# Exchanged weight groups as one transfer each, and a new pair in the shared slot

## The chip, the cores and the metric

The kernel runs on one core of a Trainium2 chip. The metric is the device time of one execution in microseconds (us). For the kernel before it is the median of three timed runs; the rows of the profile come from one further execution.

## The reference, cut to what matters

Two independent attention layers are computed and laid side by side in the output. Part A is a dilated sliding-window attention over 2048 positions. Part B, which the change touches, is a recurrent one: 2048 positions in 64 segments of 32, each with 8 memory rows in front that the segment before has made.

```python
for s in range(n_seg):                       # 64 segments
    h = concatenate([mem, xs])               # 8 memory rows + 32 rows, 640 wide
    q, k, v = h @ Wq, h @ Wk, h @ Wv         # 32 heads of 192
    p = softmax(mask(q @ k.T * scale))
    o = (p @ v) @ Wo                         # back to 640
    mem, out = o[:8], o[8:]                  # the next segment needs mem
```

Each of the four weights of part B has 640 x 6144 numbers in bf16, 7.9 MB; the four together do not fit in SBUF.

## The kernel before, in words

Part A comes first, and the weights of part B are loaded and copied while it runs. Then `segment(s)` (line 714) is called 64 times, and `project_late` (line 827) projects what was kept of the last rows.

**Groups and units.** The heads stand in four groups, 0 to 3. A group of Wq, Wk or Wv is five units `(m, g, dc)`, one for each fifth of the 640 input rows: a tile of 128 partitions x 1536 bf16, 3072 bytes in each partition, 384 KB in all. A group of Wo is six units `("o", i, 0)` of 128 x 1280, 320 KB each. Line 327 (`pieces`) lists the units of a group.

**Residents and exchanges.** Nearly all units stay in SBUF. For k, v and o, groups 0 and 3 (`SHARED`, line 305) share slots. Even segments take the groups in the order 0, 1, 2, 3 and odd ones 3, 2, 1, 0 (`TURN`, line 304). So the shared group that a segment uses first is used up early, its slots are overwritten with the other shared group, which the segment uses last and the next one first. `change` (line 376) does this with one `replace` (line 370) for each unit: the slot gets the new unit's name, and SyncE (the queue SP in the profile) issues a DMA from a copy in DRAM (`wcopy_...`, made by `copy_shared`, line 350). A DMA on SP waits until TensorE has read the old unit for the last time, and everything behind it on SP waits too.

**The pair.** `PAIR` (line 306) names two more units that share one slot: `("k", 1, 4)` and `("o", 17, 0)`, the latter belonging to group 2 of Wo. Each segment overwrites k's with o's after k of group 1 has been projected, and back after the output projection of group 2. That makes 5 + 5 + 6 + 2 = 18 weight loads in a segment.

**The order of a segment.** `ORDER` (line 294) is written out by hand and fixes the order on TensorE, VectorE, ScalarE and SP. A token is a step and the place in the turn: `k.0` projects k for the first group of the turn. Cut to the steps that the prediction uses:

```text
q.0 k.0 k.1 q.1 S.0 v.0 q.2 S.1 k.2 tp.0 v.1 q.3 mix.0 tp.1 S.2 k.3
out.0.0 v.2 out.0.1 mix.1 S.3 tp.2 v.3 mix.2 out.1.0 out.1.1 tp.3 out.2.0 out.2.1 mix.3 last ql
```

A projection (line 517, in `project32`) walks through the five units `dc`, with 4 matmuls for a unit, or 8 in the groups that a segment renews (it then projects later rows ahead). `out.0.0` multiplies the first four units of Wo of the first group (line 669), `out.0.1` the last two; `last` does all six of the last group (line 696). The first projection of the next segment, `q.0`, is preceded by `ql`.

**What SP issues in a segment, in order:** the four stores of the segment before (line 733, at `q.0`); five units of k after `k.0`; one unit of the pair after the k of group 1; the next input rows (`XS`, line 490) ahead of `v.0`; five units of v after `v.0`; six units of o after `out.0.1`; the other unit of the pair after the output of group 2. GpSimd issues the stores of `late_o` (line 654) on a queue of its own. The last segment also loads fifteen tiles of `late_o` (line 820) at `q.0`, `q.1` and `q.2`, and six units of Wo at `v.1` (line 822).

Of the kernel before, what the change touches and what calls it, by code (L numbers as in the profile page):

```python
# [8 lines left out]
BF16 = mybir.dt.bfloat16  # L9
# [293 lines left out]
SPREAD = "SSVV"  # L303
TURN = (0, 1, 2, 3), (3, 2, 1, 0)
SHARED = (0, 3)
PAIR = ("k", 1, 4), ("o", 17, 0)
LEAD_IN = 114


# [7 lines left out]
def part_b(ctx, tc, B_x, B_mem0, B_Wq, B_Wk, B_Wv, B_Wo, out, ident, n_seg, pre, mid):  # L317
    nc = tc.nc
# [8 lines left out]
    def pieces(m, g):  # L327
        if m == "o":
            return [("o", i, 0) for i in range(6 * g, 6 * g + 6)]
        return [(m, g, dc) for dc in range(5)]  # L330

    def unit_src(u):
        m, c, dc = u
        return wo_v[:, c] if m == "o" else w_in[m][:, dc, 1536 * c:1536 * c + 1536]

    def unit_cols(u):
        return 1280 if u[0] == "o" else 1536

    def two_rows(v, u):
        return v.rearrange("p (k d) -> p k d", k=2) if u[0] == "o" else v  # L340
# [7 lines left out]
    copied = {}  # L348

    def copy_shared():  # L350

        for u in [u for g in SHARED[::-1] for m in "kvo" for u in pieces(m, g)] + list(PAIR):
            copied[u] = dpool.tile([128, unit_cols(u)], BF16, name="wcopy_%s%d_%d" % u)[:]
            nc.sync.dma_start(two_rows(copied[u], u), unit_src(u))

    need = [(m, g) for m, g in (("q", 0), ("k", 0), ("q", 1), ("k", 1), ("q", 2), ("k", 2), ("v", 0), ("v", 1), ("o", 0),
                                ("q", 3), ("v", 2), ("o", 1), ("o", 2))]
    resident = [u for m, g in need for u in pieces(m, g) if u != PAIR[1]]
    res, slots, wait = {}, {}, set()

    def place_resident(pool, units):
        for u in units:
            slots[u] = pool.tile([128, unit_cols(u)], BF16, name="wres_%s%d_%d" % u)[:]
            res[u] = slots[u]

    def load_resident(units):
        for u in units:
# [2 lines left out]
    def replace(old, new):  # L370
        slots[new] = slots.pop(old)
        del res[old]
        res[new] = slots[new][:, 0:unit_cols(new)]
        nc.sync.dma_start(res[new], copied[new])

    def change(m, g):
        for old, new in zip(pieces(m, g), pieces(m, SHARED[0] + SHARED[1] - g)):
            replace(old, new)

    n_pre, used = 0, 0  # L380
    while n_pre < len(resident) and used < pre:
# [4 lines left out]
    dpool = ctx.enter_context(tc.tile_pool(name="b_copy", bufs=1, space=bass.MemoryType.DRAM))  # L386
# [4 lines left out]
    def window_rows(j):  # L391
        xj = x2[:, 160 * j:160 * j + 160].rearrange("(s n) d -> s n d", n=SEG)
        last = n_seg - 3
        return [(XW[0, j, 0:M], mem2[:, 160 * j:160 * j + 160]),
                (XA[j].rearrange("(t n) d -> t n d", n=M), xj[0:4, SEG - M:SEG]),
                (XW[1:last, j, 0:M], xj[4:n_seg, SEG - M:SEG]),
                (XW[last:n_seg, j, 0:M], xj[last:n_seg, SEG - M:SEG]),
                (XW[:, j, M:SEG], xj[:, 0:SEG - M])]

    rows = [window_rows(j) for j in range(4)]  # L400
# [87 lines left out]
    def load_x(s):  # L488
        if s < n_seg:
            nc.sync.dma_start(XS[:], XW[s].rearrange("j n c -> (j n) c"))  # L490
# [60 lines left out]
    def project_qk(s, m, g):  # L551
        return project32([ahead, main] if renewed(s, m, g) else [main], m, g)
# [13 lines left out]
    def values(s, g):  # L566
        return project32([ahead, main] if renewed(s, "v", g) else [main], "v", g)
# [146 lines left out]
    def segment(s):  # L714
        last = s + 1 == n_seg
        engine = {"S": S_, "V": V_}
        got = {}

        def project(m, g):
            if m == "v":  # L720
                got["v", g] = values(s, g)
            else:
                got[m, g] = project_qk(s, m, g)

        turn = TURN[s % 2]

        def step(name, *at):
            n = int(at[0][-1]) if at else None
            g = turn[n] if at else None
            if name in "qkv":  # L730
                if name == "q" and n == 0:
                    while stores:
                        nc.sync.dma_start(*stores.pop(0))
                if name == "v" and n == 0:
                    load_x(s + 1)
                project(name, g)
                if name != "q" and n == 0:
                    change(name, g)
                if (name, g) == PAIR[0][0:2]:
                    replace(*PAIR)  # L740
                if s == 0 and n == 0 and name != "q":
                    load_all("o", 1 if name == "k" else 2)
                if last and name == "q" and n < 3:
                    load_late(range(5 * n, 5 * n + 5))
                if last and name == "v" and n == 1:
                    load_outputs()
            elif name == "e":
                m = at[0][0]
                got["sb", m, g] = evacuate(m, got.pop((m, g)), [engine[c] for c in EVACUATE[at[0]]])
            elif name == "T":  # L750
                m = at[0][0]
                keep = fill_late(s, m, g, got.pop(("sb", m, g)))
                turn_in_place(columns_of(m, 0, 32))
                if at[0] == "k0" and s and keep:
                    got["keep"] = keep
                elif keep:
                    keep()
                if at[0] == "k1" and "keep" in got:
                    got.pop("keep")()
            elif name == "S":  # L760
                got["S", g] = scores(g)
            elif name == "sb":
                got["t", g] = soft_begin(got.pop(("S", g)))
            elif name == "mx":
                got["mx", g] = soft_max(got["t", g])
            elif name == "sub":
                soft_exp(got["t", g], got.pop(("mx", g)))
            elif name == "send":
                soft_end(s, g, got.pop(("t", g)))
            elif name == "tp":  # L770
                got["p", g] = turn_p(g)
            elif name == "PT":
                got["PT", g] = spread_p(got.pop(("p", g)), SPREAD[n])
            elif name == "ve":
                keep_values(g, got.pop(("v", g)))
            elif name == "mix":
                got["mix", g] = mix(g, got.pop(("PT", g)))
            elif name == "ot":
                keep_mix(s, g, got.pop(("mix", g)), [engine[c] for c in HEADS[n]])
            elif name == "out":  # L780
                half = int(at[1])
                if "Y" not in got:
                    got["Y"] = ps_y.tile([128, 320], FP32, tag="y", name="Y")
                n = int(at[0])
                g = turn[n]
                project_out(got["Y"], g, range(4 * half, 4 + 2 * half), n == 0, n == 2)
                if half and n == 0 and not last:
                    change("o", g)
                if half and g == PAIR[1][1] // 6 and not last:
                    replace(*PAIR[::-1])  # L790
            elif name == "part":
                got["part"] = join_begin(got["Y"])
            elif name == "join":
                join_end(got["Y"], got["part"])
                got["partT"] = None if last else turn_part(got["part"])
            elif name == "tx":
                turn_x(s + 1)
            elif name == "ql":
                got["ql"] = None if last else project32([ahead], "q", (s + 1) % 4)
            elif name == "eql":  # L800
                got["sbl"] = None if last else to_sb(got["ql"][0], S_)
            elif name == "last":
                got["Z"] = bank()[:, 0:160]
                project_last(got["Z"], turn[3])
            elif name == "close":
                close(s, got["Z"], got["part"], got["partT"])
            elif name == "Tql":
                if not last:
                    gl = (s + 1) % 4
                    turn_late(got["sbl"], "q", gl, s, s + 1)()  # L810

        for token in (ORDER if s else FIRST).split():
            step(*token.split("."))
# [4 lines left out]
    def load_late(quads):  # L818
        for b in quads:
            nc.sync.dma_start(res[DEAD[b]], late_o[b].rearrange("p g i c -> p (g i c)"))  # L820

    def load_outputs():

        for old, new in zip(pieces("k", end[1]) + pieces("v", end[1]), pieces("o", end[3])):
            replace(old, new)
# [41 lines left out]
    def load_all(m, g=None):  # L867
        for u in [u for u in pending if u[0] == m and (m != "o" or u[1] // 6 == g)]:
            load_pending(u)
# [76 lines left out]
```

## Time and profile before

| what | value |
|---|---|
| median of three runs | 1841.75 us (1837.48 to 1843.45) |
| the profiled execution | 1827.04 us |
| its span, first to last instruction | 1825.2 us |
| granted TensorE clock | 0.988 |
| matmuls on TensorE (PE) | 1631.7 us busy, 39286 matmuls |
| DMA, moved over the span | 495.96 MB, 272 GB/s |

The span is the time from the first to the last instruction of the profiled execution. PE is TensorE, and SPq marks an instruction that SP's sequencer issues, a DMA's issue above all. In a view in order of time, a row gives the start, the time from the start of the first to the end of the last instruction of the row, the engine, the line, the operation with `out<-in`, and the count; what stands in brackets is how long the engine was idle before it and what released it. In the chain of waits, a row "DMA x<-y" is a transfer from its issue to its landing, so that its start plus its duration is the time at which the data can be used. `wres_k`, `wres_v`, `wres_o` are slots in SBUF.

### The profile page before, as it was taken

How to read it: one execution, taken by the hardware profiler on the slowest of the kernel's cores; microseconds unless marked ns; L12 is line 12 of the kernel's file. 1: busy time of each engine (PE TensorE's matmuls, PEld its weight loads, DVE VectorE, ACT ScalarE, POOL GpSimd, SP SyncE). 2: the span in 40 equal slices, each digit the busy share in tenths (PEclk: the TensorE clock that was granted, in tenths of full speed). 3: DMA queues.
4: the chain of work that ended last, by engine and by line, in shares of the span. 5: the costliest groups of instructions: out<-in, count | busy, mean ns of one | idle time of the engine just before them, and what ended most of it. 6: DMA issues, size and time to landing. Idle time of an engine off the chain costs nothing.

```text
span 1825.2 us, 90715 instructions
## 1 busy us (share of the span) xinstructions
PE 1631.7 (89%) x39286; PEld 1048.1 (57%) x39286; DVE 1286.1 (70%) x3687; ACT 675.8 (37%) x1805; POOL 547.9 (30%) x1612
## 2 busy tenths in 40 slices
PE   8898989989898989898989999999899898989978
PEld 5555555555555555555555555555555555555558
DVE  4777677767777777777777777777777777777720
ACT  3454333333333333333334333333333333333310
POOL 4001233333333333333333333333333333333310
PEclk9999999999999999999999999999999999999989
DMA  9954978887777888777878887877778887777860
GB/s 315 334 158 172 332 256 288 282 290 282 256 278 273 286 291 300 263 284 254 295 271 292 300 292 274 285 280 282 277 281 290 300 291 286 276 261 276 285 264 18
DMA packets 233405, 495.96 MB, mean 272 GB/s; under 512 B 59092, under 2 KB 73410, under 8 KB 233004
## 3 DMA queue, kind: packets, MB, share of 16 engines
q1 hardware_dynamic: 222572, 478.97, 74.3%
q0 software_dynamic: 10336, 11.12, 1.9%
q8 instruction: 308, 5.05, 1.1%
q14 instruction: 93, 0.76, 0.1%
q10 hardware_dynamic: 96, 0.06, 0.0%
HBM read 475.87 MB, written 26.71 MB: 275 GB/s over the span
## 4 chain that ended last, share of the span: by engine, by line
PE 59%; DVE 16%; DMA 14%; issue 5%; ACT 4%; POOL 1%; SPq 1%; ACTq 0%; DVEq 0%; POOLq 0%
PE acc L517 30%; DMA wres_o<-wcopy_o 8%; PE px L581 6%; PE Y L669 6%; PE pq L95 3%; PE px L696 3%; PE px L644 3%; DMA wres_v<-wcopy_v 3%; PE px L620 2%; DVE QT L527 2%; DVE sb L527 1%; DMA wres_k<-wcopy_k 1%; DVE mx L594 1%; PE px L841 1%; DVE px L587 1%
## 5 line engine op out<-in xcount | busy, mean ns | idle before, releaser
L517 PEld LDWEIGHTS <-HX 128*32 128x32 bf16 x19380 | 498.7, 97 | 297.0 <-issue 60.9
L517 PE MATMUL acc<-wres_v,HX 128*32 128x384 bf16 x6460 | 324.4, 329 | 22.4 <-DMA wres_v<-wcopy_v 10.0
L517 PE MATMUL acc<-wres_q,HX 128*32 128x384 bf16 x6460 | 316.9, 328 | 3.6 <-issue 1.9
L517 PE MATMUL acc<-wres_k,HX 128*32 128x384 bf16 x6460 | 302.2, 328 | 7.7 <-DMA wres_k<-wcopy_k 3.7
L653 POOL COPY OL<-OT 128x96 bf16<-128x96 bf16 x256 | 159.0, 621 | 270.1 <-ACT OT L652 182.3
L669 PE MATMUL Y<-wres_o,OT 128*32 128x320 bf16 x4352 | 201.2, 303 | 12.9 <-issue 8.1
L563 POOL COPY QT<-Lb 128x96 bf16<-128x96 bf16 x252 | 68.3, 271 | 395.3 <-PE px L581 395.3
L652 DVE CAST OT<-px 128x240 bf16<-128x240 f32 x256 | 102.6, 401 | 118.4 <-PE px L644 108.1
L527 DVE STREAM_TRANSPOSE QT<-QT 128x384 bf16<-128x384 bf16 x256 | 146.6, 573 | 51.7 <-ACT QT L556 49.6
L556 ACT CAST KT<-acc 128x384 bf16<-128x384 f32 x192 | 92.4, 481 | 230.7 <-PE px L581 170.1
L581 PE MATMUL px<-KT,QT 64*64 64x40 bf16 (+1 forms) x4096 | 138.5, 189 | 32.8 <-issue 15.3
L652 ACT CAST OT<-px 128x240 bf16<-128x240 f32 x256 | 92.3, 361 | 191.9 <-PE px L644 104.3
L581 PEld LDWEIGHTS <-QT 64*64 64x64 bf16 (+1 forms) x4096 | 109.4, 108 | 92.6 <-issue 64.7
L570 ACT CAST Vst<-acc 128x384 bf16<-128x384 f32 x256 | 123.5, 482 | 105.1 <-PE px L644 72.7
L654 POOL DMA_DIRECT2D late_o<-OL x256 | 138.5, 541 | 75.7 <-POOL OL L653 55.8
L669 PEld LDWEIGHTS <-OT 128*32 128x32 bf16 x4608 | 113.2, 97 | 66.7 <-issue 16.9
L587 DVE SCALAR_TENSOR_TENSOR px<-px,mask 128x160 f32<-128x160 f32 x256 | 82.8, 323 | 91.8 <-PE px L581 91.8
L527 DVE STREAM_TRANSPOSE KT<-KT 128x384 bf16<-128x384 bf16 x256 | 141.5, 553 | 4.6 <-ACT KT L556 3.5
L599 ACT ACTIVATE px<-px 128x160 f32<-128x160 f32 x256 | 74.5, 291 | 165.2 <-DVE px L598 110.2
L644 PE MATMUL px<-PT,Vst 64*128 64x80 bf16 (+1 forms) x2048 | 123.2, 212 | 7.3 <-issue 4.4
L523 ACT CAST sb<-acc 128x384 bf16<-128x384 f32 x99 | 47.4, 479 | 215.3 <-PE acc L517 203.6
L547 POOL COPY Lb<-sb 128x96 bf16<-128x96 bf16 x453 | 105.2, 271 | 59.5 <-DVE sb L527 59.3
(105 smaller groups left out, 2284.8 us busy)
## 6 DMA issues: line engine op xcount, KB each, us to landing
wres_k<-wcopy_k SPq DMA_DIRECT2D x383, 384.0 KB
wres_v<-wcopy_v SPq DMA_DIRECT2D x320, 384.0 KB
wres_o<-wcopy_o SPq DMA_DIRECT2D x378, 320.0 KB
wres_k<-wcopy_o SPq DMA_DIRECT2D x69, 320.0 KB
wres_q<-in_B_Wq_dram SPq DMA_DIRECT2D x20, 384.0 KB
late_o<-OL POOLq DMA_DIRECT2D x256, 24.0 KB, 3.8
wres_q<-late_o SPq DMA_DIRECT2D x16, 384.0 KB
wres_k<-in_B_Wk_dram SPq DMA_DIRECT2D x15, 384.0 KB
```

Of the source, the lines that this page charges most:

```text
L517: nc.tensor.matmul(ps[n][32 * j:32 * j + 32].rearrange("p (f n) -> p f n", n=32), lhsT=X[:, dc, :], rhs=columns(w, (m, g, dc), j), start=( ...
L527: nc.vector.transpose(t, t)
L547: nc.gpsimd.tensor_copy(late[m, g, t][:], rows(t))
L556: copies[1](columns_of(m, 0, 32), ps[-1][:].rearrange("p (f n) -> p f n", n=32))
L570: S_(Vst[:], ps[-1][:])
L581: nc.tensor.matmul(Sps[64 * h:64 * h + 64, a, :], lhsT=QT[k0:k1, L * f:L * f + 64], rhs=KT[k0:k1, f, :], start=(outer == 0 and a == 0), st ...
L587: nc.vector.scalar_tensor_tensor(out=Sps, in0=Sps, scalar=scale, in1=mask[:].unsqueeze(1).to_broadcast([128, 4, L]), op0=ALU.mult, op1=ALU ...
L644: nc.tensor.matmul(ps[r][lo:hi, 2 * L * k:2 * L * k + 2 * L], lhsT=V[64 * r:64 * r + 64, col:col + hi - lo], rhs=PT[64 * r:64 * r + 64, 2 ...
L652: copy(OT[:, 6 * r:6 * r + 6].rearrange("p c n -> p (c n)"), ps[r][:, 0:6 * L])
L653: nc.gpsimd.tensor_copy(OL[:, g % 2].rearrange("p n c -> p c n"), OT[:, :, 32:L])
L654: nc.gpsimd.dma_start(late_o[s // 4][:, g, s % 4], OL[:, g % 2].rearrange("p n c -> p (n c)"))
L669: nc.tensor.matmul(Y[t:t + 32].rearrange("p (b c) -> p b c", b=2), lhsT=OT[:, slot(c), 0:32], rhs=quarter(w, u, 2 * r + gv), start=first a ...
```

## The change

Four edits, all in part B.

1. The DRAM copies of an exchanged group lie side by side, in one tensor of 128 rows: 15360 bytes a row for k, v and o alike (5 x 3072, 6 x 2560). Its slots in SBUF are one tile in the same way.
2. `change` renames all units of the group and then issues one DMA for them. For k and v it waits, as a whole, for the last matmul on any of the five units, and its data are there, as a whole, when all of it has landed.
3. For o there are two DMAs: the first four units after `out.0.0`, the last two after `out.0.1`.
4. The pair is now `("v", 1, 4)` and `("v", 2, 4)`, the last unit of v in groups 1 and 2. `v.1` reads one, and right behind it SP issues the load of the other, which `v.2` of the same segment reads. The next segment takes the two groups in the other order, so one load a segment does. `("k", 1, 4)` and `("o", 17, 0)` have slots of their own.

That is five weight DMAs a segment, for 5 + 5 + 6 + 1 = 17 units.

```diff
-PAIR = ("k", 1, 4), ("o", 17, 0)
+PAIR = ("v", 1, 4), ("v", 2, 4)
...
     def copy_shared():
 
-        for u in [u for g in SHARED[::-1] for m in "kvo" for u in pieces(m, g)] + list(PAIR):
+        for m, g in [(m, g) for g in SHARED[::-1] for m in "kvo"]:
+            us = pieces(m, g)
+            n = unit_cols(us[0])
+            rows = dpool.tile([128, n * len(us)], BF16, name=f"wcopy_{m}{g}")[:]
+            for i, u in enumerate(us):
+                copied[u] = rows[:, n * i:n * i + n]
+                nc.sync.dma_start(two_rows(copied[u], u), unit_src(u))
+            copied[m, g] = rows
+        for u in PAIR:
...
     def place_resident(pool, units):
         for u in units:
-            slots[u] = pool.tile([128, unit_cols(u)], BF16, name="wres_%s%d_%d" % u)[:]
-            res[u] = slots[u]
+            m, g = (u[0], u[1] // 6) if u[0] == "o" else u[0:2]
+            us = pieces(m, g) if m != "q" and g in SHARED else [u]
+            if u == us[0]:
+                n = unit_cols(u)
+                rows = pool.tile([128, n * len(us)], BF16, name="wres_%s%d_%d" % u)[:]
+                for i, v in enumerate(us):
+                    slots[v] = res[v] = rows[:, n * i:n * i + n]
...
-    def change(m, g):
-        for old, new in zip(pieces(m, g), pieces(m, SHARED[0] + SHARED[1] - g)):
-            replace(old, new)
+    def change(m, g, part=slice(None)):
+
+        other = SHARED[0] + SHARED[1] - g
+        olds, news = pieces(m, g)[part], pieces(m, other)[part]
+        for old, new in zip(olds, news):
+            slots[new] = res[new] = slots.pop(old)
+            del res[old]
...
+        n = unit_cols(olds[0])
+        a = n * pieces(m, g).index(olds[0])
+        nc.sync.dma_start(slots[m, other][:, a:a + n * len(olds)], copied[m, other][:, a:a + n * len(olds)])
...
                 if name != "q" and n == 0:
                     change(name, g)
-                if (name, g) == PAIR[0][0:2]:
-                    replace(*PAIR)
+                if name == "v" and n == 1:
+                    replace(("v", g, PAIR[0][2]), ("v", turn[2], PAIR[0][2]))
...
-                if half and n == 0 and not last:
-                    change("o", g)
-                if half and g == PAIR[1][1] // 6 and not last:
-                    replace(*PAIR[::-1])
+                if n == 0 and not last:
+                    change("o", g, slice(4 * half, 4 + 2 * half))
```

More of the change, by code (lines that the diff above doesn't have):

```diff
@@ L350, in copy_shared @@
     def copy_shared():
-        for u in [u for g in SHARED[::-1] for m in "kvo" for u in pieces(m, g)] + list(PAIR):
+        for m, g in [(m, g) for g in SHARED[::-1] for m in "kvo"]:
[7 more added lines that the diff above has]
+        for u in PAIR:
             copied[u] = dpool.tile([128, unit_cols(u)], BF16, name="wcopy_%s%d_%d" % u)[:]
-            nc.sync.dma_start(two_rows(copied[u], u), unit_src(u))
+            nc.sync.dma_start(copied[u], unit_src(u))
     need = [(m, g) for m, g in (("q", 0), ("k", 0), ("q", 1), ("k", 1), ("q", 2), ("k", 2), ("v", 0), ("v", 1), ("o", 0),
@@ L362, in place_resident @@
         for u in units:
-            slots[u] = pool.tile([128, unit_cols(u)], BF16, name="wres_%s%d_%d" % u)[:]
-            res[u] = slots[u]
+            m, g = (u[0], u[1] // 6) if u[0] == "o" else u[0:2]
[5 more added lines that the diff above has]
+                    slots[v] = res[v] = rows[:, n * i:n * i + n]
+                if len(us) > 1:
+                    slots[m, g] = rows
     def load_resident(units):
@@ L374, in replace @@
         nc.sync.dma_start(res[new], copied[new])
-    def change(m, g):
-        for old, new in zip(pieces(m, g), pieces(m, SHARED[0] + SHARED[1] - g)):
-            replace(old, new)
+    def change(m, g, part=slice(None)):
[4 more added lines that the diff above has]
+            del res[old]
+        if (m, g) in slots:
+            slots[m, other] = slots.pop((m, g))
+        n = unit_cols(olds[0])
+        a = n * pieces(m, g).index(olds[0])
+        nc.sync.dma_start(slots[m, other][:, a:a + n * len(olds)], copied[m, other][:, a:a + n * len(olds)])
     n_pre, used = 0, 0
```

## The prediction

> **What bounds the kernel now.** I read the page's head and its chain first, for what sets the end.
>
> ```profile
> span 1825.2 us, 90715 instructions
> PE 1631.7 (89%) x39286; PEld 1048.1 (57%) x39286; DVE 1286.1 (70%) x3687; ACT 675.8 (37%) x1805; POOL 547.9 (30%) x1612
> ...
> PE 59%; DVE 16%; DMA 14%; issue 5%; ACT 4%; POOL 1%; SPq 1%; ACTq 0%; DVEq 0%; POOLq 0%
> ```
>
> TensorE is busy for 89% of the span and carries 59% of the chain. The chain's 14% of DMA is not what faster loads would give: a transfer on the chain stands there from issue to landing, most of it beside busy matmuls. What can be won is TensorE's idle time that a DMA ended. So next the waits of TensorE, between 250 and 1725 us, the 61 or so segments that look alike (us in total, times, longest).
>
> ```profile
> PE px L581 <- issue: 14.9, 35, 0.9
> PE px L644 <- issue: 11.3, 13, 1.9
> PE Y L669 <- issue: 9.8, 11, 1.7
> PE acc L517 <- DMA wres_v<-wcopy_v: 8.2, 14, 1.3
> PE px L696 <- DMA wres_o<-wcopy_o: 6.0, 13, 1.3
> PE px L696 <- issue: 5.1, 9, 1.7
> ```
>
> All that TensorE loses to weight loads there is 8.2 + 6.0 = 14.2 us. **The most that the change can win in the steady part is 14 us**, under 1% of the time. So what counts is whether it adds a wait. I therefore went through two segments in order of time. SP's issues in the odd segment that starts near 659 us, and in the even one near 1605 us:
>
> ```profile
> 661.70 2.25 SPq L374 DMA_DIRECT2D wres_k<-wcopy_k  x5
> 664.61 5.72 SPq L374 DMA_DIRECT2D wres_v<-wcopy_v  x5
> 671.00 0.32 SPq L374 DMA_DIRECT2D wres_k<-wcopy_o  x1
> ...
> 1608.22 2.25 SPq L374 DMA_DIRECT2D wres_k<-wcopy_k  x5
> 1610.56 0.38 SPq L374 DMA_DIRECT2D wres_k<-wcopy_o  x1
> 1611.46 4.80 SPq L374 DMA_DIRECT2D wres_v<-wcopy_v  x5
> 1619.17 2.70 SPq L374 DMA_DIRECT2D wres_o<-wcopy_o  x6
> ```
>
> and TensorE's rows of the same segments: v.1 (20 matmuls), v.2 (40 and 20), the rows behind v.2, and v.3, whose last four wait for the last unit of v.
>
> ```profile
> 667.69 1.00 PE L517 MATMUL acc<-wres_v,HX 128*32 128x384 bf16 x20
> 672.71 1.81 PE L517 MATMUL acc<-wres_v,HX 128*32 128x384 bf16 x40
> 674.33 0.46 PE L669 MATMUL Y<-wres_o,OT 128*32 128x320 bf16 x8
> 677.20 0.35 PE L517 MATMUL acc<-wres_v,HX 128*32 128x384 bf16 x4 [0.53 <-DMA wres_v<-wcopy_v]
> ...
> 1614.86 1.00 PE L517 MATMUL acc<-wres_v,HX 128*32 128x384 bf16 x20
> 1619.36 0.99 PE L517 MATMUL acc<-wres_v,HX 128*32 128x384 bf16 x20
> 1620.17 0.45 PE L669 MATMUL Y<-wres_o,OT 128*32 128x320 bf16 x8
> 1621.45 0.54 PE L581 MATMUL px<-KT,QT 64*64 64x40 bf16 x16 [0.39 <-issue]
> 1623.17 0.35 PE L517 MATMUL acc<-wres_v,HX 128*32 128x384 bf16 x4 [0.20 <-DMA wres_v<-wcopy_v]
> ```
>
> The chain has the landings of those last units of v (start, duration):
>
> ```profile
> 670.01 7.15 DMA wres_v<-wcopy_v
> ...
> 1615.94 7.18 DMA wres_v<-wcopy_v
> ```
>
> A load of 384 KB issued at 670.01 landed 7.15 us later, at 677.16: it stood in the queue behind the loads of k and v before it. The ten units of k and v took 677.16 - 661.70 = 15.5 us from k's first issue in the one segment, and 1623.12 - 1608.22 = 14.9 us in the other, with a unit of o among them.
>
> **The change part by part.**
>
> *The new pair.* It takes away two loads of a segment (one of 384 KB, one of 320 KB) and adds one of 384 KB with a deadline: it is issued when v.1 has been read (about 668.6 and 1615.8) and v.2 needs it for its last unit, after four fifths of v.2. From the start of v.2's row to that of out.0.1 behind it these are 672.71 + 4/5 of 1.62 = 674.0 and 1619.36 + 4/5 of 0.81 = 1620.0. SP's queue serves it behind k and v. The price of one unit more in a full queue is seen in the last segment, where v.3 waits for unit after unit:
>
> ```profile
> 1750.61 0.35 PE L517 MATMUL acc<-wres_v,HX 128*32 128x384 bf16 x4 [0.62 <-DMA wres_v<-wcopy_v]
> 1751.58 0.35 PE L517 MATMUL acc<-wres_v,HX 128*32 128x384 bf16 x4 [0.62 <-DMA wres_v<-wcopy_v]
> 1752.56 0.35 PE L517 MATMUL acc<-wres_v,HX 128*32 128x384 bf16 x4 [0.64 <-DMA wres_v<-wcopy_v]
> ```
>
> That is 0.98 us a unit. So at today's pace the pair lands at 677.16 + 0.98 = 678.1, 4.1 us after 674.0; and at 1623.12 - 0.82 (the unit of o in front is gone, 0.98 x 320/384) + 0.98 = 1623.3, 3.3 us after 1620.0.
>
> *Rows of 15360 bytes.* No transfer of before has them. From below the gain is nothing. For the other side the rate in the queue while it is full (907 to 919 us, and 1742 to 1760 us; the last row is the second stretch in 40 slices):
>
> ```profile
> DMA packets 1700, 4.27 MB, mean 356 GB/s; under 512 B 309, under 2 KB 309, under 8 KB 1698
> ...
> DMA packets 2758, 7.23 MB, mean 402 GB/s; under 512 B 331, under 2 KB 363, under 8 KB 2756
> GB/s 403 396 362 430 410 430 396 399 427 389 430 396 416 389 396 417 396 403 410 396 410 396 396 403 419 394 376 389 369 403 413 406 401 423 395 388 412 394 381 404
> ```
>
> The engines run at 402 GB/s in the mean and 430 in the best slices. If long rows hold 430 throughout, ten units (3.93 MB) take 9.1 us in place of 9.8: 0.7 us. If they also undo what makes an ordinary segment slower than the saturated one (356 GB/s, 11.0 us), it is 1.9 us. I take 0.7, since the rest has no sign of coming from the length of a row. The Trainium skill ("DMA: Bandwidth & Descriptors", Rules for kernel authors) tells authors to coalesce many small transfers into one large one, and fits a DMA by 2.0 us plus its bytes over 436 GB/s (Anatomy of one DMA, the GpSimd path); by that fit the pair would land 2.9 us after its issue, in time. The 7.15 us of the chain for that size is against it here: the fit leaves out the queue.
>
> *One DMA for a group.* k's DMA waits for the last matmul of k.0 and no longer for the first: in segments where k.0 has 20 matmuls, SP's four stores end later than that anyway, so nothing; where it has 40, some 0.3 us. v's DMA is issued at v.0's end, while k still flows: nothing. That k.3 and v.3 get their group as a whole costs nothing beside the pair, which comes last in the queue: what lets v.2 go has let v.3 go. SP saves issues, and TensorE never waits for SP alone.
>
> *The sum for the pair.* The two segments give 4.1 - 0.7 = 3.4 and 3.3 - 0.7 = 2.6 us, plus up to 0.3. They are late ones, though: their v.3 waited, and in the whole stretch only 14 did. From below: in the segment of 907 to 919 us, which waited for nothing, the 4.27 MB of the row above are ten units, the one of o and the input rows but for a few packets, so v was through near 918.5 for the mean engine, the pair at 918.5 + 0.98 - 0.7 = 918.8, and v.2 needs it at 918.44 + 0.65 = 919.1:
>
> ```profile
> 918.44 0.99 PE L517 MATMUL acc<-wres_v,HX 128*32 128x384 bf16 x20
> 921.22 1.00 PE L517 MATMUL acc<-wres_v,HX 128*32 128x384 bf16 x20
> ```
>
> with a landing lag of the slowest engine, that is about 0.5 us of wait; from above, its v.3 (from 921.22, last four 0.65 later) didn't wait, so 921.9 + 0.98 - 0.7 - 919.1 = 3.1 us. Between 0.5 and 3.4 I take **2.0 us a segment**, times 62 = 124 us.
>
> *What takes up some of it.* Behind v.2 TensorE idles anyway: 0.39 us before S.3 in the row at 1621.45, 14.9 us in all by the waits (35 times); these go, since S.3's inputs don't wait for v.2. The other issue waits behind v.2 (11.3 + 9.8 + 5.1 = 26.2 us) are put at half, 13, between none and all. Off: 28 us.
>
> *Outputs asked sooner.* This edit moves a call, not an issue: SP had nothing else to do, and each load waited for its own matmuls alone, so the first of o goes out at 1619.17 already, before out.0.1. As a block of four it goes out when out.0.0 has ended, 0.2 us later, and only the pair is new in front of it. From the pair's 1622.6 the six units take 5 us, 1627.5, well before `last` (some 8 us after v.2). The 6.0 us of wres_o and the 8.2 of wres_v go: 14 us off.
>
> *First and last segment.* In the first, the pair is queued behind the six first loads of group 2 of Wo; the loads issued near there land 6.7 us later, near 207.5, and v.2 needs it at 203.8:
>
> ```profile
> 202.39 1.91 PE L517 MATMUL acc<-wres_v,HX 128*32 128x384 bf16 x40
> ...
> 206.47 6.72 DMA wres_o<-wcopy_o
> ```
>
> about 3 us. In the last it stands behind fifteen tiles of late_o. I put that at 3 us too, between nothing, since the waits at v.3 above go when v.2 waits, and the 11 us by which it would land after v.2's need if it came about 8 us behind the last of those rows. Together 6 us.
>
> **Sum:** 124 - 28 - 14 + 6 = +88 us on the profiled execution (1825.2 of span and 1.8 around it): 1915 us. That execution is 15 us below the median of the three runs; I put the same 88 us on the median: 1841.75 + 88 = **1930 us**.
>
> **The rivals.**
>
> ```profile
> 906.22 2.29 SPq L374 DMA_DIRECT2D wres_k<-wcopy_k  x5
> GB/s 61 72 256 266 420 379 440 379 399 348 358 358 246 246 246 328 396 430 379 341 396 364 387 430 399 444 420 369 420 379 410 389 420 399 420 408 439 405 345 253
> ...
> q8 instruction: 308, 5.05, 1.1%
> ```
>
> The first two rows are k's issue and the rate from 907 us on in slices of 0.3 us: the data flow 1.4 us after the issue.
>
> 1. *The pair comes in time* (faster). The mechanism: long rows keep all engines at their best rate, with no laggard. At 430 GB/s from 1.4 us after k's issue (1609.6), k, v and the input rows (3.97 MB) take 9.2 us and the pair 0.9: 1619.7, just before 1620.0. It decides at 10.4 us from k's first data to the pair. Then 14 us are won and a few lost at the ends: about 1831 us. For it: single slices do reach 430. Against: the saturated stretch, with nothing to wait for, holds 402, and this segment needed 14.9 us. Chance 0.13.
> 2. *A little late*: 0.5 us a segment, the lower end. 31 - 10 - 14 + 5 = +12: 1854 us. Chance 0.10.
> 3. *Long rows hold up what shares the engines*, above all instruction fetches, whose lateness shows as "issue" waits (41 us in the rows above). An engine busy with a row of 15360 bytes (0.57 us at a sixteenth of 430 GB/s, against 0.11) lets others in later. The last row has 308 packets of instructions in the span, some 4 a segment; if each comes 0.25 us later and nothing hides it, +62 over the forecast: about 1990 us. The Trainium skill ("DMA: Bandwidth & Descriptors", Queues, rings and completion order) has an engine switch between queues only at packet boundaries, which speaks for this one; no trace of before shows its size. Chance 0.08.
> 4. *The halves of o are not told apart*, so that out.0.1 waits for the load issued at out.0.0, some 6 us a segment: above 2100 us. The kernel before already has writes and reads of parts of one tile (`KT`) side by side. Chance 0.03.
>
> **How the numbers follow.** The forecast has 0.66; its own range is 1880 to 1975 (stalls of 1.2 to 2.8 us). The range of 8 in 10 goes from 1850, which takes in rival 2, to 1990: left out are rivals 1 and 4 and the tails. A measurement of this kernel can tell about 0.3% (5.5 us) from no change: faster by more 0.13, within 0.04 (the edges of rivals 1 and 2), slower 0.83.
>
> **What would show it.** The waits of TensorE after the change: a new row at line 517 for the pair's load into `wres_v`, some 60 times, 1 to 3 us each, ended in v.2's last four or eight matmuls, and no wait for wres_o. In the chain, DMA rows for the pair from v.1's end, of 5 to 8 us. The steady segment becomes 25.6 us where it is 24.3 (k's issues at 661.70 and 1608.22 lie 39 segments apart). If v.2 does not wait, step one was wrong: then rival 1. If it waits but for under 1 us, the rate of long rows was undervalued. If issue waits double, rival 3.

## The result, and the profile after

| | before | after |
|---|---|---|
| median | 1839.62 us (1831.31 to 1843.45, 4 runs) | 1937.1 us (1928.64 to 1942.62, 4 runs) |
| ratio, 95% interval | 1 | 1.0532 (1.0475 to 1.059) |
| span of the profiled execution | 1825.2 us | 1940.8 us |
| its granted TensorE clock | 0.988 | 0.958 |

The changed kernel is 5.3% slower, 97.5 us by the medians of one comparison. The two profiled executions lie further apart (115.6 us of span), since before's lies 12.6 us under this median and after's 5.5 above.

The page of after, with the rows that answer to those of before: head, busy time, bytes moved, the chain's shares, and the group of v's matmuls (busy us, mean ns of one | idle before it, and what ended most of it).

```profile
span 1940.8 us, 89121 instructions
PE 1658.4 (85%) x39286; PEld 1045.0 (54%) x39286; DVE 1292.9 (67%) x3687; ACT 674.9 (35%) x1805; POOL 547.1 (28%) x1612
...
DMA packets 114304, 475.22 MB, mean 245 GB/s; under 512 B 45860, under 2 KB 60178, under 8 KB 89468
...
PE 56%; DMA 25%; DVE 11%; ACT 4%; issue 3%; POOL 1%; SPq 0%; ACTq 0%; DVEq 0%; POOLq 0%
...
L541 PE MATMUL acc<-wres_v,HX 128*32 128x384 bf16 x6460 | 359.4, 350 | 161.3 <-DMA wres_v<-wcopy_v 147.1
```

Three things are to be seen. TensorE is idle for 1940.8 - 1658.4 = 282.4 us, where it was 1825.2 - 1631.7 = 193.5: 88.9 us more. The same 39286 matmuls keep it busy 26.7 us longer, and the mean matmul of v has become 350 ns long, from 329, while its shape is what it was. And 475 MB were moved in place of 496, fewer bytes in more time. 88.9 + 26.7 = 115.6 us is the whole difference of the spans.

What ended the idle time, from the waits of TensorE over the whole span (us in total, times, longest):

```profile
PE acc L541 <- DMA wres_v<-wcopy_v: 147.1, 62, 10.8
...
PE acc L541 <- issue: 10.7, 17, 1.3
...
PE acc L541 <- DMA wres_k<-wcopy_k: 6.6, 2, 6.1
...
PE Y L693 <- issue: 4.3, 5, 1.4
```

All rows of the view that a DMA ended, part A's among them, come to 163.7 us here, and to 39.3 us in the same view of before: +124.4. Those that ended in "issue" come to 15.5 us, and to 48.1 in before: -32.6. Waits for other engines are 82.9 and 82.8 us. 124.4 - 32.6 + 0.1 = 91.9 accounts for the 88.9 us of idle time but for 3 us, by which short gaps that the view doesn't list have shrunk. No wait for `wres_o` is left.

One segment in order of time, SP first. It is the whole weight traffic of a segment:

```profile
926.54 0.35 SPq L402 DMA_DIRECT2D wres_k<-wcopy_k  x1
927.07 1.35 SPq L514 DMA_DIRECT2D XS<-xwindows  x1
929.70 0.32 SPq L402 DMA_DIRECT2D wres_v<-wcopy_v  x1
933.57 0.32 SPq L389 DMA_DIRECT2D wres_v<-wcopy_v  x1
937.19 5.26 SPq L402 DMA_DIRECT2D wres_o<-wcopy_o  x2
```

TensorE in v.2 and just behind it, and the chain's row for the pair:

```profile
936.97 1.64 PE L541 MATMUL acc<-wres_v,HX 128*32 128x384 bf16 x32
941.30 0.51 PE L541 MATMUL acc<-wres_v,HX 128*32 128x384 bf16 x8 [2.69 <-DMA wres_v<-wcopy_v]
...
943.03 1.75 PE L541 MATMUL acc<-wres_v,HX 128*32 128x384 bf16 x20
```
```profile
933.57 7.70 DMA wres_v<-wcopy_v
```

The pair is issued when v.1 has ended and lands 7.70 us later, at 941.27. v.2 has done its first 32 matmuls at 938.61 and stands until 941.30. The next row of v, v.3, is 20 matmuls in 1.75 us; before, 20 took 1.00. The windows around it tell why (us, then busy of PE, PEld, DVE, ACT and POOL, granted clock, DMA share, GB/s):

```profile
941.00:943.00 2.00, 1.70 (x50) 1.14 (x49) 0.32 (x1) 0.37 (x2) 0.00 (x0) 1.00 0.62 249
943.00:946.40 3.40, 3.40 (x54) 1.69 (x56) 2.17 (x9) 1.04 (x3) 1.15 (x2) 0.52 0.69 221
946.40:950.00 3.60, 2.97 (x106) 1.96 (x102) 2.54 (x8) 1.68 (x5) 1.91 (x4) 0.98 0.04 11
```

1.7 us after the stall the granted clock falls to half for 3.4 us, with TensorE busy throughout. In the last row the queue is dry, at 11 GB/s: what was issued has landed, and the next weights are issued in the next segment.

The steady segment: the first and the last issue of k between 250 and 1725 us lie 55 segments apart.

```profile
271.10 0.35 SPq L402 DMA_DIRECT2D wres_k<-wcopy_k  x1
...
1711.93 0.35 SPq L402 DMA_DIRECT2D wres_k<-wcopy_k  x1
```

1440.83 / 55 = 26.2 us, where it was 24.3.

### The profile page after: what moved, and what is told of

It is laid out like the page before. It is cut to its first block, busy times and chain, and to the rows that moved or that the text cites. A ratio compares the mean times of both kernels' runs of the same rounds, so it can differ in the third digit from the quotient of the medians.

```text
span 1940.8 us, 89121 instructions
## 1 busy us (share of the span) xinstructions
PE 1658.4 (85%) x39286; PEld 1045.0 (54%) x39286; DVE 1292.9 (67%) x3687; ACT 674.9 (35%) x1805; POOL 547.1 (28%) x1612
## 4 chain that ended last, share of the span: by engine, by line
PE 56%; DMA 25%; DVE 11%; ACT 4%; issue 3%; POOL 1%; SPq 0%; ACTq 0%; DVEq 0%; POOLq 0%
PE acc L541 29%; DMA wres_v<-wcopy_v 23%; PE Y L693 7%; PE px L605 4%; PE px L720 3%; PE px L668 3%; PE pq L95 3%; PE px L644 2%; ACT QT L700 1%; PE px L863 1%; DVE prod L151 1%; ACT OT L676 1%; DVE OT L676 1%; PE acc L863 1%; DVE mx L618 1%
## 5 line engine op out<-in xcount | busy, mean ns | idle before, releaser
L541 PE MATMUL acc<-wres_v,HX 128*32 128x384 bf16 x6460 | 359.4, 350 | 161.3 <-DMA wres_v<-wcopy_v 147.1
L693 PE MATMUL Y<-wres_o,OT 128*32 128x320 bf16 x4608 | 218.4, 314 | 6.8 <-issue 4.3
L668 PEld LDWEIGHTS <-Vst 64*128 64x128 bf16 (+1 forms) x2048 | 62.3, 101 | 107.6 <-issue 55.8
```

The costliest lines, as they stand in the source:

```text
L541: nc.tensor.matmul(ps[n][32 * j:32 * j + 32].rearrange("p (f n) -> p f n", n=32), lhsT=X[:, dc, :], rhs=columns(w, (m, g, dc), j), start=( ...
L668: nc.tensor.matmul(ps[r][lo:hi, 2 * L * k:2 * L * k + 2 * L], lhsT=V[64 * r:64 * r + 64, col:col + hi - lo], rhs=PT[64 * r:64 * r + 64, 2 ...
L693: nc.tensor.matmul(Y[t:t + 32].rearrange("p (b c) -> p b c", b=2), lhsT=OT[:, slot(c), 0:32], rhs=quarter(w, u, 2 * r + gv), start=first a ...
```

## The experiments

**The theory:** the pair's unit is the last of eleven in SP's queue and is needed before the five units of v that stand in front of it, so TensorE stands in v.2 until it lands; a part is given back behind the stall, and a part is lost again to the clock that follows it. **Rivals:** the grouping is at fault (one landing for a group; long rows that hold up instruction fetches); or the clock is most of the loss, and the stall itself little.

### The old pair, with everything else of the change

```diff
-PAIR = ("v", 1, 4), ("v", 2, 4)
+PAIR = ("k", 1, 4), ("o", 17, 0)
...
-                if name == "v" and n == 1:
-                    replace(("v", g, PAIR[0][2]), ("v", turn[2], PAIR[0][2]))
+                if (name, g) == PAIR[0][0:2]:
+                    replace(*PAIR)
...
+                if half and g == PAIR[1][1] // 6 and not last:
+                    replace(*PAIR[::-1])
```

> The changed kernel with the old pair (one unit of k with one of o, both swapped back each segment); groups in one transfer with long rows and the two halves of o stay. If the new pair is the cause of the loss, its wait in v.2 is gone and the time is back at that of before: 1830 to 1855 us, with at most a few tenths of a us a segment at v.3, which now waits for its group as a whole. If the single long transfers are the cause (waiting for whole groups, or holding up other traffic), it stays above 1900 us.

Measured: 1841.77 us, ratio to before 1.0029 (1.0003 to 1.0054), as expected of the pair as the cause. The waits between 250 and 1725 us:

```profile
PE Y L693 <- issue: 20.2, 20, 2.1
PE acc L541 <- issue: 13.0, 23, 1.1
PE px L668 <- issue: 12.7, 14, 1.4
PE px L605 <- issue: 12.1, 23, 1.5
PE px L720 <- DMA wres_o<-wcopy_o: 5.6, 11, 0.8
PE px L720 <- issue: 5.6, 10, 0.9
PE acc L541 <- DMA wres_v<-wcopy_v: 4.1, 7, 0.9
```

With the old pair the loss is gone but for 0.3%. The waits for weights are a little under before's 14.2 us, and those for "issue" 64 us, 17 above the 47.7 of before in the same stretch. Grouping, long rows and halves together neither cost nor win much; the pair does it.

### The new pair alone, in the kernel before

```diff
-PAIR = ("k", 1, 4), ("o", 17, 0)
+PAIR = ("v", 1, 4), ("v", 2, 4)
...
-                if (name, g) == PAIR[0][0:2]:
-                    replace(*PAIR)
+                if name == "v" and n == 1:
+                    replace(("v", g, PAIR[0][2]), ("v", turn[2], PAIR[0][2]))
...
-                if half and g == PAIR[1][1] // 6 and not last:
-                    replace(*PAIR[::-1])
```

> The kernel before with the new pair alone; one transfer for each unit, rows of 3072 and 2560 bytes. If the pair is the cause and long rows help it a little, the pair lands some 0.7 us later than in the changed kernel and the time is 1950 to 1990 us. If the long transfers are the cause, it is within 1840 to 1870 us.

Measured: 1994.01 us, ratio 1.0834 (1.0778 to 1.0889), a little above what was expected. The clock and the wait of the steady part (250 to 1725 us):

```profile
core 0: 1999.1 us, clock 0.940
```
```profile
PE acc L517 <- DMA wres_v<-wcopy_v: 148.2, 55, 4.3
```

and the wait of after in the same stretch:

```profile
PE acc L541 <- DMA wres_v<-wcopy_v: 120.2, 54, 3.8
```

148.2 / 55 = 2.7 us a wait, against 120.2 / 54 = 2.2 in after, and a clock that is lower still. So the grouped transfers with their long rows help, by 0.5 us a segment. Which of the two helps can't be told from these two kernels, which differ in both; the experiment with short rows bears on it. The excess over the expectation is in busy time: 1686.2 us by this kernel's page, 54.5 over before.

### The pair ahead of a part of v

v is issued as three units behind `v.0`; then, behind `v.1`, the pair, and after it the last two units.

```diff
                 if name != "q" and n == 0:
-                    change(name, g)
+                    change(name, g, slice(0, 3) if name == "v" else slice(None))
                 if name == "v" and n == 1:
                     replace(("v", g, PAIR[0][2]), ("v", turn[2], PAIR[0][2]))
+                    change("v", turn[0], slice(3, 5))
```

> The changed kernel with the group of v in two transfers: three units after v.0, then the pair's load, then the last two units. The pair is issued at the same time as before, but with two units (about 1.9 us) fewer in front of it. If it waits for its place in the queue, the wait in v.2 falls from 2.3 to under 0.8 us a segment, the half-clock stretches mostly go, and the time is 1840 to 1880 us. If the load takes its 6 to 7 us from issue whatever is ahead, it stays at 1925 to 1945 us.

Measured: 1839.59 us, ratio 1.0025 (0.9998 to 1.0051), just under the first range. The waits of the steady part, and the chain's row of a pair (start, duration):

```profile
PE acc L541 <- DMA wres_v<-wcopy_v: 30.8, 35, 2.1
PE px L720 <- DMA wres_o<-wcopy_o: 9.6, 14, 1.1
```
```profile
958.00 6.07 DMA wres_v<-wcopy_v
```

The same 17 units, the same long rows, the same pair: two units of v fewer in front of it take 5.1% off (1.0532 to 1.0025). The place in the queue is the cause, not the pair as such.

### The pair ahead of more of v

The same with two units of v in front and three behind the pair (`slice(0, 2)`, `slice(2, 5)`).

> As with the pair ahead of the last two units of v, but ahead of the last three. By the queue the pair lands another 0.95 us earlier and the gap in v.2 falls from 0.74 to about 0.2 us a segment. If what is won there is not lost at v.3, whose last three units now land after the pair, the time falls by 10 to 25 us against that run, to 1815 to 1830 us. If the wait only moves to v.3, or the time was never in that wait, it stays at 1830 to 1850 us.

Measured: 1885.97 us, ratio 1.0268 (1.0222 to 1.0313). The expectation failed. In the one-microsecond windows around the pair's issue, first here, then in the kernel with three units in front (last two columns: DMA share, GB/s):

```profile
956.00:957.00 1.00, 1.00 (x32) 0.51 (x24) 0.97 (x4) 0.27 (x2) 0.68 (x4) 1.00 0.69 287
957.00:958.00 1.00, 0.83 (x26) 0.57 (x20) 0.78 (x4) 0.57 (x2) 0.22 (x2) 1.00 1.02 124
```
```profile
957.00:958.00 1.00, 1.00 (x29) 0.67 (x32) 0.93 (x5) 0.93 (x3) 0.00 (x0) 1.00 0.96 377
958.00:959.00 1.00, 1.00 (x32) 0.51 (x28) 0.86 (x4) 0.29 (x1) 0.00 (x0) 1.00 0.98 411
```

Here the rate falls to 287 and then 124 GB/s just when pair and rest are issued (956.15 and 956.52 by SP's rows): what stood in front was through, and the engines had little until the new issues flowed. (The share of 1.02 counts the packets that start in the window at their full length, and the first ones behind the gap are long.) The other kernel, issuing at 958.00 and 958.37, keeps 377 and 411. So it is in the mean of the steady segments too: between 8 and 10 us after k's issue the packets bring 280 and 194 GB/s here, and 424 and 334 there.

In v.2 the expectation came true: the waits there are 8.8 us in the steady part, where they were 30.8. But the three units that now start later are late for v.3, as in this row, and o behind them for `last`:

```profile
964.55 1.15 PE L541 MATMUL acc<-wres_v,HX 128*32 128x384 bf16 x12 [0.94 <-DMA wres_v<-wcopy_v]
```

The steady part has 51.8 us of waits for `wres_v`, 43 of them at v.3, and 25.2 for `wres_o`. By these two kernels the queue should be kept full up to the pair's issue, and no fuller.

### Matmuls of zeros in the wait

Two kernels add 48, or 24, matmuls in v.2 ahead of its last unit, with an operand of zeros, which adds nothing to the sum. They fill the time in which TensorE stood, and so tell what the clock costs.

```diff
+            for _ in range(fill if dc == 3 else 0):
+                for j in range(4):
+                    nc.tensor.matmul(ps[0][32 * j:32 * j + 32].rearrange("p (f n) -> p f n", n=32), lhsT=zero[:],
+                                     rhs=columns(w, (m, g, dc), j), start=False, stop=False, tile_position=(0, 32 * j))
```

48 matmuls:

> The changed kernel with 48 more matmuls (12 rows of four, with weights of zero, about 2.0 us) between the fourth and the fifth unit of v.2, where TensorE waits; they add zeros, so the sums stay. If TensorE's idle time in the wait is what halves its granted clock for 3.4 us, the half-clock stretches fall from 43 to under 15 and the time falls by 20 to 35 us, to 1902 to 1918 us, though there is more work. If the clock falls for another reason (load, traffic, time), the stretches stay and the time is 1935 to 1950 us.

24 matmuls:

> The changed kernel with 24 matmuls of zeros in the wait (about 1.0 us) in place of 48. The wait is 2.4 us in the mean, so they fit into it nearly always and cost nothing by themselves; the idle rest is 1.4 us. If only idle stretches above some 2.2 us halve the clock, the half-clock stretches fall from 43 to under 15, and without the longer gap of the run with 48 (2.65 us against 2.44) the time is 1905 to 1920 us. If shorter idle stretches do it too, more than 25 stay and the time is 1925 to 1940 us.

Measured: 48 matmuls 1927.46 us, ratio 1.0497 (1.046 to 1.0533), some 10 us over the upper end expected; 24 matmuls 1916.2 us, ratio 1.0431 (1.0397 to 1.0465), within the first range expected. The waits of the kernel with 48 (whole span), then TensorE's rows of one v.2 with 24:

```profile
PE acc L544 <- DMA wres_v<-wcopy_v: 23.1, 22, 8.2
PE acc L548 <- issue: 14.3, 20, 1.2
PE acc L544 <- issue: 13.1, 19, 2.1
PE px L676 <- issue: 5.6, 8, 1.2
```
```profile
955.48 0.82 PE L544 MATMUL acc<-wres_v,HX 128*32 128x384 bf16 x16
956.12 1.15 PE L548 MATMUL acc<-wres_v,zero 128*32 128x384 bf16 x24
958.63 0.35 PE L544 MATMUL acc<-wres_v,HX 128*32 128x384 bf16 x4 [1.36 <-DMA wres_v<-wcopy_v]
```

The stretches at half clock, 43 in after, are 8 with 48 matmuls and 15 with 24 (just not the "under 15" expected), though there is more work: they come from TensorE's idle time. With 24, the idle stretch shown is 1.36 us in place of 2.69, the mean clock is 0.983, and the time is 1.0% lower than after's, 18.6 us by the ratios (6 to 31 by their intervals), with more instructions on TensorE: about that much at least the falls of the clock cost.

With 48 the clock is 0.988, before's, but the ratio is only 0.35% lower, which is within the noise. The filling took 1.15 us for 24 matmuls and so 2.3 for 48, about the stall's mean length and so more than it where the pair came early, and the waits for "issue", 15.5 us in after, are back at 36.6, 14.3 of them ahead of the filling itself. The two kernels stay 5.0 and 4.3% above before: the stall itself, not the clock, is most of the loss.

### Short rows with the old pair

The copies of the first experiment's kernel lie unit behind unit, so that the same single transfers have rows of 3072 and 2560 bytes.

```diff
-            rows = dpool.tile([128, n * len(us)], BF16, name=f"wcopy_{m}{g}")[:]
+            rows = dpool.tile([len(us), 128, n], BF16, name=f"wcopy_{m}{g}")
...
-                copied[u] = rows[:, n * i:n * i + n]
+                copied[u] = rows[i]
```

> Old pair, one transfer for a group, but the copies lie unit behind unit, so that a row of the transfer is 3072 or 2560 bytes again. With long rows the old pair took 1.003 of the time of before, its DMA waits were lower by some 9 us and its issue waits on TensorE higher (63 against 47 us from 250 to 1725 us). If long rows hold up the fetch of instructions, the issue waits are back under 52 us here and the time is at or below that of before (0.990 to 1.001). If they rose for another reason, they stay near 60 us and the ratio at 1.000 to 1.006.

Measured: 1851.25 us, ratio 1.0069 (1.0038 to 1.0101). The waits of the steady part:

```profile
PE acc L542 <- DMA wres_v<-wcopy_v: 15.0, 21, 1.1
PE Y L694 <- issue: 14.2, 16, 1.5
```

Short rows bring 11 us more of waits for `wres_v` (15.0 against 4.1); the waits for "issue", of which the largest row is shown, come to 58.4 us against 64.5. The ratio is a little above the second range expected. So long rows hold up nothing that shows in the time. They win a little, 0.4% by the two ratios, which lies at the edge of the noise.

### o as one transfer, with the old pair

This is the first experiment's kernel, with all six units of o issued after `out.0.1`.

```diff
-                if n == 0 and not last:
-                    change("o", g, slice(4 * half, 4 + 2 * half))
+                if half and n == 0 and not last:
+                    change("o", g)
```

> Old pair and long rows, with o in one transfer after out.0.1 in place of two. The prediction held that the edit moves a call and no bytes that anything waits for. If so, the ratio to before stays within 0.003 of the run with two halves (1.0029), so 1.000 to 1.006. If the four units that go out earlier matter, last waits longer for wres_o (over 20 us in all where it was 5.6) and the ratio is above 1.008.

Measured: 2018.4 us, ratio 1.1003 (1.0961 to 1.1045). The first case of the expectation, that nothing changes, is out; the second holds, and goes far beyond its bounds. TensorE's waits over the whole span, and then the one ahead of a `last`, with the transfer in SP's row and the chain's:

```profile
PE px L720 <- DMA wres_o<-wcopy_o: 165.9, 60, 3.9
```
```profile
977.80 1.01 PE L720 MATMUL px<-wres_o,OT 128*32 128x160 bf16 x48 [2.79 <-DMA wres_o<-wcopy_o]
```
```profile
969.61 0.32 SPq L402 DMA_DIRECT2D wres_o<-wcopy_o  x1
```
```profile
969.61 8.05 DMA wres_o<-wcopy_o
```

The one transfer goes out when `out.0.1` has ended, at 969.61, and all of its 1920 KB must be there before `last` starts, which would have been at 975.0. It lands at 977.66. In before the first units were issued ahead of `out.0.1`. The Trainium skill ("DMA: Bandwidth & Descriptors", Rules for kernel authors) has authors coalesce many small transfers into one large one, and calls those under 64 KB mostly overhead. Here 1280 and 640 KB were joined, and the larger one costs nearly 10%, since its first byte waits for the last reader of the old weights and its reader for the last byte. Some of the loss comes by way of the clock, which is 0.941 here and 0.984 with two transfers.

### A smaller exchange for the pair

A slot of 2432 columns holds both units of the old pair but for 384 columns, and each exchange overwrites only these: 96 KB in place of 384 and 320.

```diff
+            if u == PAIR[0]:
+                both = pool.tile([128, 2432], BF16, name="wres_%s%d_%d" % u)[:]
+                res[u], res[PAIR[1]] = both[:, 0:1536], both[:, 1152:2432]
+                continue
...
+    def swap(new):
+        a = 1152 if new == PAIR[0] else 0
+        nc.sync.dma_start(res[new][:, a:a + 384], copied[new][:, a:a + 384])
...
```

In the kernel before:

> The kernel before, but the old pair shares only the last 384 of k's 1536 columns with the first 384 of o's: the two views overlap in one tile, and the two swaps move 96 KB each in place of 384 and 320. Nothing gets a nearer deadline and 0.5 of 6.6 MB a segment go. If DMA waits are worth what the waits of TensorE say (14 us in the steady part, of which this saves about half), the ratio is 0.992 to 0.998. If what is saved there comes back as issue waits, as with long rows, it is 0.998 to 1.003.

Measured: 1826.12 us, ratio 0.9952 (0.9925 to 0.998), as expected, and a little faster than before. And for the new pair (2688 columns), in the kernel that issues it ahead of two units of v:

> The pair ahead of the last two units of v, and the two units of v overlap in one tile by 384 columns, so that its load moves 96 KB in place of 384. By the queue the pair and the rest of v land 0.7 us earlier: the gap in v.2 goes from 0.74 to 0.1 us a segment. If that wait is what the run without overlap still lost, the ratio to before falls from 1.0025 to 0.985 to 0.997. If the stall was being paid back behind v.2, where issue waits shrink when TensorE stalls, it stays at 0.998 to 1.004.

Measured: 1841.29 us, ratio 1.0035 (1.0004 to 1.0067), the second case of the expectation. The waits of the steady part, first of the one, then of the other:

```profile
PE px L707 <- DMA wres_o<-wcopy_o: 7.6, 16, 0.9
...
PE acc L528 <- DMA wres_v<-wcopy_v: 2.9, 6, 0.7
```
```profile
PE px L730 <- DMA wres_o<-wcopy_o: 29.5, 33, 2.5
...
PE acc L551 <- DMA wres_v<-wcopy_v: 4.5, 11, 0.9
```

With the small exchange v.2 hardly waits for the new pair, 4.5 us against 30.8, but `last` waits for o in its place, 29.5 against 9.6, and the waits for "issue" are 42.5 us against 28.9. o comes no later: in the mean of the steady segments its last packets end 20.1 us after k's issue, and 20.0 without the overlap, while TensorE is ready for `last` at 19.1 in place of 19.4. It comes no earlier either, though less lies in front of it. Between 12 and 14 us after k's issue the rate is 237 and 230 GB/s, where it was 359 and 278, which fits a queue that runs low before o's data flow; no run tests this.

## Why the prediction was right, point by point

The forecast was 1930 us, +88 us; measured were 1937.1 us and +97.5 by the medians. Its mechanism held, and the 88 us are met almost to the microsecond by the idle time of TensorE: +88.9. That they meet so closely is luck: the 2.0 us of a segment were taken between bounds of 0.5 and 3.4, and the waits came out 8 us higher and what is given back for them 5 us higher. What the forecast had no term for is the other 26.7 us of the spans, in which TensorE is busy. The medians hide most of this, since before's profiled execution was a quick one: 1915 us were forecast for the profiled execution, and it took 1942.6.

- **The new pair, 2.0 us a segment (124 us) and 6 us at the ends.** Right in place, cause and size. It was said to land at 678.1 and 1623.3 less 0.7, which is 15.7 and 14.4 us after k's first issue; in the segment of after it landed 941.27 - 926.54 = 14.7 us after it, 2.7 us late for v.2. The 62 segments between the first and the last waited 134 us, 2.2 each. With the 14 us off for the old waits the forecast is a net 116 us of waits for DMAs; measured +124.4. The lower bound of 0.5 us holds a lag of the slowest engine, 0.8 us from 918.8 on, for which the prediction shows no row. At the ends the first segment waited 2.15 us, where 3 were put. In the last one v.2 waited 10.8 us, and there the upper bound of 11 was the better figure. The 6.1 us for `wres_k` in the same segment are not the pair's doing, since they are 5.5 with the old pair. Before lost 9.9 us to weights in its last segment, so that the net there is +7, where 3 were put.
- **Rows of 15360 bytes, 0.7 us.** Right in size: the kernels with and without the long transfers differ by 0.5 us a wait. How much of it is due to the rows alone is not shown.
- **One DMA for a group costs nothing beside the pair.** Held: with the old pair the three other edits cost 0.3% together, and all waits for `wres_v` in the steady part are 4.1 us. In after all 62 waits for `wres_v` are in v.2 and none is at v.3, as the prediction said.
- **What takes up some of it, 28 us.** Right: the waits for "issue" fell by 32.6 us. The prediction had the gap before S.3 go whole and half of the rest; of its four rows, 41.5 us in the whole span, 4.8 are left, while the waits ahead of the projections rose from 5.8 to 10.7.
- **Outputs asked sooner: "This edit moves a call, not an issue".** True against the six loads of before. But it was used to put the edit at nothing, and within this change that is wrong: once o is grouped, the halves are what holds the load's first byte early, and without them the kernel is at 1.1003 and not at 1.0029.
- **The waits for `wres_o` and the old one for `wres_v` go, 14 us.** Right: the row for `wres_o` is gone, and so are the waits at v.3.
- **The sum.** 130 - 28 - 14 = +88 against +124.4 - 32.6 = +91.8 in the waits. To that comes the clock, which the prediction doesn't mention: after stalls of this length it falls to half for 3.4 us. It adds 26.7 us of busy time, of which the shorter filling shows some 18.6 us (6 to 31) to be time lost.

The rivals: *the pair in time* and *a little late* are out by the 62 waits of 147.1 us. *Long rows hold up what shares the engines*, at 62 us over the forecast, is out by the short rows (1.0069 against 1.0029, in the other direction) and by the "issue" waits of after, which fell. *The halves not told apart* is out: there is no wait for `wres_o` in after.

Of the signs, the steady segment came out at 26.2 us against 25.6; the clock takes some 0.8 us in 36 of 62 segments (below), which is 0.5 a segment. The row at v.2, its count of about 60, its 1 to 3 us (six of the steady waits lie outside, the longest at 3.8) and the chain's rows of 5 to 8 us (5.3 to 8.5 in the steady part) were as said.

## What to carry to other kernels

A load that is needed soon must not be queued behind loads that can wait: count the bytes in front of it and the time until its reader comes, and put it ahead of what can wait, but only as early as the queue still has work in front of it. Two units that share a slot between two uses in the same segment leave the exchange only the time between these uses; overlapping the two in all but a strip makes the exchange small, and with the old pair that gained 0.5%, with the new one nothing. A large transfer starts when its last old reader has ended and serves when its last byte is there, so it is worth splitting wherever readers come one after another.

## What the hardware showed that was not expected

**A short stall costs more than its length.** In after's trace the granted clock is at half in 43 stretches, 39 of them of 3.41 us, in before's in 9. Stalls of 2.2 to 3 us in v.2 were enough: the one shown is 2.69 us, with the clock at 0.52 from 943.0 to 946.4 behind it. From v.2's last unit to the next segment's first matmul with Wq it takes 8.5 us in the median of the 36 steady segments that have such a stretch, and 7.7 in the 26 without. The Trainium skill ("TensorE: Matmul & The Clock Gate", HAM oscillation — how this bites in real kernels) asks for no idle gaps of TensorE above about 3.4 us; the length of the stretch agrees with that figure, but here the shorter stalls did it, most but not all of the time.

The trace tells when. All 43 stretches begin on one grid with a step of 3.41 us. What counts is TensorE's idle time, short gaps included, within one step of that grid. Between 250 and 1720 us, every one of 20 steps with over 1.9 us idle was followed by half clock, 13 of the 23 with 1.4 to 1.9 us, and none of the 305 with less (steps at half clock themselves left out). With the new pair alone it is 33 of 33, 9 of 18 and none of 279. A segment of 26.2 us is no multiple of 3.41, so the stall wanders over the grid: one of 2.86 us, from 753.8 on, is cut by it into 1.60 and 1.26, and the clock stayed full.

**A stall gives "issue" time back.** Waits for "issue" are 48.1 us in before and 15.5 in after. Kernels with the same matmuls line up: between 250 and 1725 us the waits for DMAs and for "issue" are 120.6 and 14.2 us in after, 40.6 and 28.9 with the pair ahead of two units of v, 21.8 and 58.4 with short rows and the old pair, 9.7 and 64.5 with long rows and the old pair. The less TensorE stands for data, the more it waits for instructions. That its instructions catch up meanwhile fits; no run here takes it apart further.
